# A tuned kernel for a long convolution and a linear attention block: other chunks, another transpose of the filter, 16-tile stages, work on GpSimd, and a new order

## The chip, the cores and the metric

The kernel runs on one core of one Trainium2 chip. The metric is the device time of one launch in microseconds (us). Engines are called as in the profile: PE (TensorE), DVE (VectorE), ACT (ScalarE), POOL (GpSimd) and SP (SyncE, which issues the DMAs). All data is bf16, and PE adds up in f32 in PSUM, which has eight banks.

## The reference

Two independent blocks share one output of 2048 x 1152, A in the left half and B in the right half. S = 2048 positions, D = 576 channels.

```python
k_shift = sum(k_pad[:, t:t + S, :] * shift_k[:, ks - 1 - t] for t in range(4))    # A: a 4-tap convolution
kv = k_shift * v
y = irfft(rfft(kv, 2 * S) * rfft(ssm_k, 2 * S))[:S]                               # a causal convolution of length S
a = q * (y + kv * ssm_D)
q, k, v = split(x @ wqkv)                                                         # B: 32 heads of 18 channels
pq, pk = phi(q), phi(k)          # phi(t) = t + 1 if t > 0 else exp(t), + 1e-6
o = (pq @ (pk^T v)) / (pq . sum(pk) + 1e-6)                                       # for each head
b = o @ wo
```

## The kernel before, in words

**Order.** Every piece of work is an `Op` with a number, registered by `P.op` in program order. `PLAN` (line 811) then lists all operations with the engine that runs each (P, A, D, G, S for PE, ACT, DVE, POOL, SP); `_issue` (104) and the loop at 793 to 805 issue them in that order, so each engine works through its list in order, and an operation that waits holds up what is behind it on its engine. `PLACES` fixes the SBUF offset or PSUM bank of every buffer. All DMAs go through `dma` (239) on the one SP queue, in order too. The costs given to `P.op` and the `bias` have no effect once the list is fixed.

**Block A.** The convolution over 4096 points is made of two small transforms, 128 by 16. `conv_piece` (373) makes kv on DVE in six pieces (three chunks of 192 channels, two halves of the positions): two products of 3,072 elements per partition (L383), additions (388, 391) and the product with v (394). `h_piece` (405) loads the filter 96 channels at a time, turns it on PE (416) and adds D (425). `s1` (434) is the first transform: for the filter (h) and for kv (u), per chunk four groups of matmuls with the table Gsb (445), each evicted by `copy` (246 to 250, so L248 is ACT and L250 is DVE) to Ch or Cu. `s2` (458) takes 64 channels (nine groups): a 32x32 block transpose on DVE (463), then two groups of eight 32x32 matmuls (476), each evicted to `sph` or `spu`. `inv` (492) swaps the even and odd partitions of the filter's spectrum by two DMAs (X), makes two products on DVE (500, 503), and then runs the inverse small transform on 32x32 tiles (513), evicted to V. `inv2` (525) writes V to DRAM in two halves (320 and 256 channels) and reads it back in another order, each half by 16 DMAs of 160 or 128 KB (540); the last matmuls use the table Esb (550), DVE multiplies by q (555), and four DMAs store each half.

**Block B.** x is loaded and turned by eight DMA transposes (299, 302) in four groups of 512 positions, xT. `kproj` (569) makes 128 rows of k by ten matmuls of 288 columns (577), an exponential on ACT (582), and phi on DVE (585). `qproj` (590) makes q transposed in chunks of seven heads, 126 channels, and a last one of 72 (599, 603, 606), to pqT. x is loaded again as x_sb (621), and `b_G` (630) computes G = x^T pk by 160 matmuls (636), from which kv and z of each head follow (673, 689); M = kv wo for each chunk of heads (732). The denominator goes over `dmm` (705) and a reciprocal on DVE (723); `b_bc` (740) spreads it by matmuls (747) and DVE multiplies pqT by it in ten operations (753). `b_out` (759) multiplies pqT by M, ten matmuls for 128 rows (766), evicts to `ob` and stores.

```python
    for b, p in zip([b for b in P.bufs if b.space != "dram"], places, strict=True):
        b.pos = p
...
            o.fn(o.eng)
```

Of the kernel before, what the change touches and what calls it, by code (L numbers as in the profile page):

```python
# [13 lines left out]
S = 2048  # L14
# [4 lines left out]
HEADS = [7, 7, 7, 7, 4]  # L19
CC = 192  # L20
NCC = 3
PCH = 64
VN = (320, 256)
VP = (0, 5)
HALF = 288

# [92 lines left out]
def _tables():  # L119
# [11 lines left out]
    pp = np.arange(128)  # L131
    k2p = 32 * (pp % 4) + pp // 4
    phe = ((4 * k2p[:, None, None] - 1) * n.T[None, :, :]) % 8192
# [21 lines left out]

    C = np.zeros((128, 96 + 128 + 630 + 32 + 160 + 126 + 8), np.float32)
    o = 0
    C[:, 0:96] = np.tile(W.reshape(32, 96), (4, 1))
    o = 96
    C[:, o:o + 128] = np.eye(128)  # L160
    o += 128
    es = np.zeros((32, 5, 126), np.float32)
    hm = np.zeros((128, 5, 32), np.float32)
    for c, (h0, hn) in enumerate(HCH):
        for m in range(hn):
            es[7 * c + m // 18, c, m] = 1.0
            hm[m, c, 7 * c + m // 18] = 1.0
    C[:, o:o + 630] = np.tile(es.reshape(32, 630), (4, 1))
    o += 630
    C[127, o:o + 32] = 1.0  # L170
    o += 32
    C[:, o:o + 160] = hm.reshape(128, 160)
    o += 160
    m = np.arange(126)
    C[:126, o:o + 126] = (m[:, None] // 18 == m[None, :] // 18)
    o += 126
    C[:, o:o + 8] = EPS
# [30 lines left out]
def kernel(  # L208
# [22 lines left out]
    V_d = [nc.dram_tensor("v_scr%d" % i, (128, 32 * VN[i]), BF, kind="Internal").ap() for i in range(2)]  # L231
# [39 lines left out]
    pqT = SB("pqT", [128, 5, S], side=1, pre=True)  # L271
# [8 lines left out]
    esel = lambda: cs(224, 630).rearrange("p (c m) -> p c m", c=5)  # L280
    sel127 = lambda: cs(854, 32)
    hmask = lambda: cs(886, 160).rearrange("p (c m) -> p c m", c=5)
    maskbd = lambda: cs(1046, 126)
    epsc = lambda: cs(1172, 1)

    P.op(("POOL", 0.1), lambda e: nc.gpsimd.memset(neg1.t[:], -1.0), wr=[neg1], name="neg1", bias=1000)
    for wx in (wk, wq):
        P.op(("POOL", 0.4), lambda e, wx=wx: nc.gpsimd.memset(wx.t[0:64, 4, :], 0.0), wr=[(wx, "z")], name="wz", bias=990)
        P.op(("POOL", 0.4), lambda e, wx=wx: nc.gpsimd.memset(wx.t[0:1, 4, :], 1.0), rd=[(wx, "z")], wr=[(wx, "z")],
             name="w1", bias=980)  # L290

    xTg = []

    def xt_load(g):
        b = SB("xT%d" % g, [128, 5, 512])
        xTg.append(b)

        def f1(e):
            nc.sync.dma_start_transpose(out=b.t[:, 0:4, :], in_=x[512 * g:512 * g + 512, 0:512])  # L299

        def f2(e):
            nc.sync.dma_start_transpose(out=b.t[:, 4:5, :], in_=x[512 * g:512 * g + 512, 448:576])
        load("xT", b, f1, 524288, wr=[(b, "m")], issue=3.3, row=256)
        load("xTt", b, f2, 131072, wr=[(b, "t")], issue=1.25, row=256)
        P.op(("POOL", 0.6), lambda e: nc.gpsimd.memset(b.t[0:1, 4, :], 1.0), rd=[(b, "t")], wr=[(b, "t")],
             name="xT1", bias=900)
# [13 lines left out]
    khs, vs = [], []  # L320

    def kv_load(bh):
        b0 = 8 * bh
        kh = SB("kh%d" % bh, [128, 11, D])
        vt = SB("v%d" % bh, [128, 8, D])
        khs.append(kh)
        vs.append(vt)
        if bh == 0:
            P.op(("POOL", 1.0), lambda e: nc.gpsimd.memset(kh.t[0:1, 0:3, :], 0.0), wr=[(kh, "z")], name="khz",
                 bias=970)  # L330
            for ci, (c0, cn) in enumerate(((0, CC), (CC, D - CC))):
                load("khh", kh, lambda e, c0=c0, cn=cn: dma(kh.t[1:16, 0:3, c0:c0 + cn], ap(
                    k, 13 * D + c0, [[16 * D, 15], [D, 3], [1, cn]])), 90 * cn, wr=[(kh, (ci, "h1"))], row=2 * cn)
                load("khh", kh, lambda e, c0=c0, cn=cn: dma(kh.t[16:128, 0:3, c0:c0 + cn], ap(
                    k, 253 * D + c0, [[16 * D, 112], [D, 3], [1, cn]])), 672 * cn, wr=[(kh, (ci, "h2"))],
                     row=2 * cn)
                load("kh0", kh, lambda e, c0=c0, cn=cn: dma(kh.t[:, 3:11, c0:c0 + cn], ap(
                    k, c0, [[16 * D, 128], [D, 8], [1, cn]])), 2048 * cn, wr=[(kh, (ci, "m"))], row=2 * cn)
        else:
            load("kh1", kh, lambda e: dma(kh.t[:], ap(k, 5 * D, [[16 * D, 128], [D, 11], [1, D]])), 1622016,  # L340
                 wr=[(kh, "m")])
        load("v%d" % bh, vt, lambda e: dma(vt.t[:], ap(v, b0 * D, [[16 * D, 128], [D, 8], [1, D]])), 1179648, wr=[(vt, "v")])
# [16 lines left out]
    kv_load(0)  # L359
    xt_load(0)  # L360
# [6 lines left out]
    load("Gsb", Gsb, lambda e: dma(Gsb.t[:].rearrange("p a b c -> p (a b c)"), G_d), 1048576)  # L367
    load("Drow", Drow, lambda e: dma(Drow.t[:], A_ssm_D.rearrange("(o d) -> o d", o=1)), 1152)


    m = SB("m", [128, 4, 8, CC])

    def conv_piece(cc, bh):
        kh, vt = khs[bh], vs[bh]
        c0 = cc * CC

        def tap(e, i):
            base = kh.t[:, i:i + 8, c0:c0 + CC]
            i0 = bass.AP(tensor=base.tensor, offset=base.offset,
                         ap=[list(base.ap[0]), [D, 2], [D, 8], [1, CC]])  # L380
            w = Wj.t[:, 2 - i:4 - i, c0:c0 + CC]
# [500 lines left out]
```

## Time and profile before

| what | value |
|---|---|
| median of 3 runs (lowest, highest) | 198.97 us (196.22, 200.73) |
| span of the profiled execution, first to last instruction | 197.3 us |
| mean granted PE clock in it | 0.895 |
| ACT, POOL busy | 120.0 us, 6.9 us |
| DMA | 39.49 MB, mean 200 GB/s |

The profile records one execution. Its own time as the runs count it isn't given apart from the span; the median of the runs lies 1.7 us above the span. Busy is the time in which an engine had an instruction at work. A group line gives the source line, the engine, the operation, output <- input, the shape, the count, the busy time, the mean of one in ns, and the idle time of the engine just before the group with what ended it. A chain line gives start, duration and what it was.

### The profile page before, as it was taken

The numbers are of one execution on the slowest core, as the hardware profiler recorded it, in microseconds if no ns is written. First come the engines' busy times: TensorE is split into PE (matmuls) and PEld (weight loads), VectorE is DVE, ScalarE is ACT, GpSimd is POOL, SyncE is SP. The second block draws the span as 40 slices with busy tenths as digits, with TensorE's granted clock in tenths as the row PEclk, the third lists the DMA queues.
The fourth block names the chain that finished last, engine by engine and source line by source line (L and its number), as shares of the span: only waits on it lengthen the run. The fifth ranks groups of instructions, "written<-read, shape, count | busy, mean of one in ns | idle before, by whom it ended". The sixth has DMA issues, their size and how long they took to land.

```text
span 197.3 us, 3955 instructions
## 1 busy us (share of the span) xinstructions
PE 162.8 (83%) x1664; PEld 108.2 (55%) x1664; DVE 153.4 (78%) x150; ACT 120.0 (61%) x127; POOL 6.9 (3%) x18
## 2 busy tenths in 40 slices
PE   0985999938999999889998897798779999996820
PEld 0763576627666675668775564362233566774610
DVE  0477599999799999999954999979899548482650
ACT  2293566595767576997524699979998583201100
POOL 8010100020010000000000000000000000000000
PEclk9996699985999999999999999769555699999996
DMA  6999899996013680209950021930699789967696
GB/s 182 348 171 262 307 379 382 300 230 138 0 22 118 201 279 17 92 3 278 372 233 0 3 106 69 308 108 0 257 342 257 187 240 360 354 189 211 198 323 185
DMA packets 40536, 39.49 MB, mean 200 GB/s; under 512 B 13575, under 2 KB 37765, under 8 KB 39622
## 3 DMA queue, kind: packets, MB, share of 16 engines
q1 hardware_dynamic: 40518, 39.24, 64.7%
q8 instruction: 13, 0.21, 0.5%
q14 instruction: 5, 0.04, 0.1%
HBM read 22.46 MB, written 9.44 MB: 162 GB/s over the span
## 4 chain that ended last, share of the span: by engine, by line
PE 37%; DVE 24%; ACT 12%; SPq 11%; issue 7%; DMA 6%; DVEq 1%; ACTq 0%
PE ps_all L636 8%; SPq L240 7%; PE ps_all L599 6%; PE ps_all L577 6%; PE ps_all L766 6%; DVE m L383 5%; PE ps_all L445 5%; DMA Vt<-v_scr 3%; ACT Cu L248 3%; DVE X L500 3%; SPq L299 2%; DVE pk L585 2%; DVE ct L463 2%; DMA wk<-in_B_wqkv_dram 2%; PE ps_all L550 2%
## 5 line engine op out<-in xcount | busy, mean ns | idle before, releaser
L445 PEld LDWEIGHTS <-Gsb 128*128 128x128 bf16 x240 | 20.0, 113 | 11.2 <-issue 9.7
L577 PE MATMUL ps_all<-wk,xT 128*128 128x288 bf16 x160 | 23.4, 306 | 2.5 <-DMA wk<-in_B_wqkv_dram 2.5
L766 PE MATMUL ps_all<-M,pqT 126*128 126x288 bf16 (+1 forms) x160 | 23.5, 305 | 0.2 <-ACT V L248 0.2
L599 PE MATMUL ps_all<-xT,wq 128*126 128x512 bf16 (+1 forms) x100 | 23.5, 386 | 0.1
L383 DVE TENSOR_TENSOR m<-kh,Wj 128x3072 bf16<-128x3072 bf16 x12 | 20.7, 1750 | 1.9 <-DMA kh<-in_A_k_dram 1.9
L577 PEld LDWEIGHTS <-xT 128*128 128x128 bf16 x160 | 16.4, 104 | 9.3 <-issue 3.6
L766 PEld LDWEIGHTS <-pqT 126*128 126x128 bf16 (+1 forms) x160 | 16.4, 103 | 7.5 <-issue 2.2
L636 PE MATMUL ps_all<-pk,x_sb 128*128 128x288 bf16 (+1 forms) x160 | 20.4, 286 | 0.1
L248 ACT ACTIVATE sph<-ps_all 128x1024 bf16<-128x1024 f32 x16 | 16.2, 1028 | 4.4 <-PE ps_all L476 4.4
L248 ACT ACTIVATE spu<-ps_all 128x1024 bf16<-128x1024 f32 x16 | 15.9, 1028 | 4.7 <-PE ps_all L476 4.7
L248 ACT ACTIVATE Cu<-ps_all 128x1536 bf16<-128x1536 f32 x12 | 17.5, 1502 | 1.1 <-PE ps_all L445 1.0
L582 ACT ACTIVATE ek<-ps_all,neg 128x576 bf16<-128x576 f32 x16 | 11.8, 741 | 10.5 <-PE ps_all L577 6.9
L636 PEld LDWEIGHTS <-x_sb 128*128 128x128 bf16 x160 | 15.5, 98 | 4.8 <-issue 0.9
L599 PEld LDWEIGHTS <-wq 128*126 128x126 bf16 (+1 forms) x100 | 13.1, 135 | 8.3 <-issue 1.3
L248 ACT ACTIVATE Ch<-ps_all 128x1536 bf16<-128x1536 f32 x11 | 16.1, 1523 | 2.5 <-PE ps_all L445 2.3
L248 ACT ACTIVATE ob<-ps_all 128x576 bf16<-128x576 f32 x10 | 6.5, 652 | 17.7 <-PE ps_all L766 17.3
L445 PE MATMUL ps_all<-hT,Gsb 128*128 128x192 bf16 (+2 forms) x120 | 12.8, 272 | 5.3 <-DVE hT L425 3.4
L476 PE MATMUL ps_all<-ct,cst 32*32 32x512 bf16 x288 | 13.2, 438 | 4.0 <-ACT Cu L248 0.9
L603 ACT ACTIVATE eq<-ps_all,neg 126x1024 bf16<-126x1024 f32 (+1 forms) x10 | 11.1, 1114 | 7.8 <-PE ps_all L599 7.8
L248 ACT ACTIVATE V<-ps_all 128x1024 bf16<-128x1024 f32 x14 | 13.7, 1035 | 2.7 <-PE ps_all L513 2.7
L555 DVE TENSOR_TENSOR q<-ps_all,q 128x640 bf16<-128x640 f32 (+1 forms) x12 | 11.0, 953 | 5.5 <-PE ps_all L550 4.6
L585 DVE SCALAR_TENSOR_TENSOR pk<-ek,ps_all 128x576 bf16<-128x576 bf16 x16 | 11.6, 746 | 3.7 <-ACT ek L582 2.0
(69 smaller groups left out, 224.1 us busy)
## 6 DMA issues: line engine op xcount, KB each, us to landing
X<-sph SPq DMA_DIRECT2D x18, 256.0 KB, 2.8
v_scr<-V SPq DMA_DIRECT2D x1, 2560.0 KB, 10.0
Vt<-v_scr SPq DMA_DIRECT2D x16, 160.0 KB, 3.5
hs<-in_A_ssm_k_dram SPq DMA_DIRECT2D x6, 384.0 KB, 5.6
v<-in_A_v_dram SPq DMA_DIRECT2D x2, 1152.0 KB, 11.1
x_sb<-in_B_x_dram SPq DMA_DIRECT2D x1, 2304.0 KB, 9.5
out_dram<-ob SPq DMA_DIRECT2D x16, 144.0 KB, 3.3
v_scr<-V SPq DMA_DIRECT2D x1, 2048.0 KB
```

The lines of the kernel that those rows point to most:

```text
L240: nc.sync.dma_start(out=dst, in_=src)
L248: nc.scalar.activation(out=o, in_=i, func=ACTF.Copy)
L383: nc.vector.tensor_tensor(out=m.t[:, i:i + 2], in0=i0, in1=i1, op=ALU.mult)
L445: nc.tensor.matmul(ps.t[:, bank, lo - 512 * bank:hi - 512 * bank], lhsT=Gsb.t[:, b, ri, :], rhs=src[:, lo - CC * j:hi - CC * j], start=Tru ...
L476: nc.tensor.matmul(ps.t[32 * j:32 * j + 32, kk, :].rearrange("p (k w t) -> p w k t", w=8, t=2), lhsT=W2()[32 * kh:32 * kh + 32, :], rhs=ct ...
L577: nc.tensor.matmul(ps.t[:, hh, 0:HALF], lhsT=xT.t[:, t, 128 * (r % 4):128 * (r % 4) + 128], rhs=wk.t[:, t, HALF * hh:HALF * hh + HALF], st ...
L582: P.op(("ACT", _act(576) + 0.085), lambda e: nc.scalar.activation(out=eb.t[:], in_=ps.t[:, :, 0:HALF], func=ACTF.Exp, bias=neg1.t[:]), rd= ...
L585: P.op(("DVE", _dve(576)), lambda e: nc.vector.scalar_tensor_tensor(out=pk.t[:, r, 0:D].rearrange("p (h c) -> p h c", h=2), in0=eb.t[:], s ...
L599: nc.tensor.matmul(ps.t[0:hn, j, :], lhsT=wq.t[:, t, h0:h0 + hn], rhs=xT.t[:, t, :], start=(t == 0), stop=(t == 4))
L603: P.op(("ACT", _act(1024) + 0.09), lambda e: nc.scalar.activation(out=eb.t[0:hn], in_=ps.t[0:hn], func=ACTF.Exp, bias=neg1.t[0:hn, :]), rd ...
L636: nc.tensor.matmul(ps.t[:, hh, 0:n], lhsT=x_sb.t[:, r, FT[t]:FT[t] + 128], rhs=pk.t[:, r, HALF * hh:HALF * hh + n], start=(r == 0), stop=( ...
L766: nc.tensor.matmul(ps.t[:, hh, 0:HALF], lhsT=pqT.t[0:hn, c, 128 * r:128 * r + 128], rhs=M.t[0:hn, c, HALF * hh:HALF * hh + HALF], start=(c ...
```

## The change

- **x** (`x_load`, `xt_load`): x_sb is loaded at the start in four parts. Groups 0 and 1 of xT are turned on PE from x_sb (XPE = 2) and evicted by ACT or DVE; groups 2 and 3 still by DMA transposes.
- **Convolution**: pieces of 128 channels (HP), the last of 64; all four tap products in one instruction; k and v are kept in one buffer each.
- **Filter**: pieces of 128 channels. For pieces 1 to 4 (HDMA) the transpose between s1 and s2 is a DMA transpose from SBUF to SBUF, 512 KB for 64 channels (seven of them), followed by two times two matmuls over all 128 partitions (W2q); piece 0 keeps the block transposes on DVE. The filter's loads for these pieces permute channels.
- **16-tile stages**: s2 and i1 run their 32x32 matmuls over all 16 tiles of the array in one operation (16 and 32 matmuls).
- **Spectral products**: each may run on DVE or POOL; the new plan puts nine of eighteen on POOL.
- **Inverse**: V goes in groups of 256, 256 and 64 channels. The first two (DR) are evicted to U, written to DRAM and read back by four DMAs of 512 KB. The third has no DRAM trip: its inverse matmuls use the data as the stationary side (i1s), so that the result lies as i2 wants it.
- **Block B**: phi in halves (kproj by 288 columns, qproj by 512); q in chunks of 128 channels that straddle heads, the 64-channel tails of two position groups packed into one tile (pqt); M in six parts, each the sum of two head chunks; bc in nine parts, of which four (PQG) are copied out by ACT or DVE and multiplied on POOL, which also adds EPS (`pqe`); G and out evicted by halves.
- **Fillers**: `FILL` puts 62 matmuls of 256 columns over zeros ahead of chosen operations, into a bank that the operation writes afterwards.
- **Plan**: new PLAN and PLACES. SP's order starts with cst, srow, the first filter piece, Gsb, Drow, a part of wk, x (first part), the head of k, wk, k, v, x (second part), wq, k (second half), x (third), then xT of group 2.

The core of the diff (PLAN, PLACES and most repeated lines left out):

```diff
+HP = [(0, 128), (128, 128), (256, 128), (384, 128), (512, 64)]
+QG = [(0, 256), (256, 256), (512, 64)]
 HALF = 288
+XPE = 2
+HDMA = (1, 2, 3, 4)
+DR = (0, 1)
...
+        if g < XPE:
+            for t in range(5):
+                ps = psb(1, "xps") if t % 2 == 0 else ps
+                c0 = 128 * t if t < 4 else D - 128
+
+                def tr(e, t=t, ps=ps, c0=c0):
+                    o = ps.t.rearrange("p b c -> p (b c)").bitcast(BF)
+                    for j in range(4):
+                        nc.tensor.transpose(out=o[:, 512 * (t % 2) + 128 * j:512 * (t % 2) + 128 * j + 128],
+                                            in_=x_sb.t[:, 4 * g + j, c0:c0 + 128], identity=ident())
+                P.op(("PE", 4 * 0.065), tr, rd=[(x_sb, g), cst], wr=[(ps, t % 2)], use=[b], name="xtr", cnt=4,
...
+            w = Wj.t[:, 3:4, c0:c0 + n]
+            i1 = bass.AP(tensor=w.tensor, offset=w.offset, ap=[list(w.ap[0]), [-D, 4], [0, 8], [1, n]])
+            nc.vector.tensor_tensor(out=m.t[:], in0=i0, in1=i1, op=ALU.mult)
...
+            cq = SB("cq", [128, 16, S // 16])
+            P.op(("SP", 3.0), lambda e, g=g, cq=cq: nc.sync.dma_start_transpose(
+                out=cq.t[:], in_=C.t[:, 16 * g:16 * g + 16].rearrange("p w r t -> p (w r t)")),
+                rd=[C], wr=[cq], name="trq", tx=_dma(524288, 256), bias=(nm, 0.0))
+            for hh in range(2):
+                ps = psb(2, "s2ps")
+
+                def mm(e, hh=hh, ps=ps, cq=cq):
+                    for k in range(2):
+                        nc.tensor.matmul(ps.t[:, k, :], lhsT=W2q(), rhs=cq.t[:, 8 * hh + 4 * k:8 * hh + 4 * k + 4, :],
+                                         start=True, stop=True)
+                P.op(("PE", _pe(512, 512)), mm, rd=[cq, cst], wr=[ps], use=[sp], name="s2q", cnt=2, bias=(nm, 0.0))
...
+        ps = [psb(2, "s2ps") for _ in range(2)]
+
+        def mm(e):
+            for j in range(4):
+                for kh in range(4):
+                    nc.tensor.matmul(ps[kh // 2].t[32 * j:32 * j + 32, kh % 2, :], lhsT=W2()[32 * kh:32 * kh + 32, :],
+                                     rhs=ct.t[32 * kh:32 * kh + 32, 8 * j:8 * j + 8], start=True, stop=True)
+        P.op(("PE", T16), mm, rd=[ct, cst], wr=ps, use=[sp], name="s2" + sfx, bias=bias, cnt=16)
...
+        for x, wr in ((1, [(tx, ("x", 0)), (tx, ("x", 1))]), (0, [(tx, 0), (tx, 1)])):
+            P.op({"DVE": _dve(2048, 2), "POOL": TPOOL}, lambda e, x=x: (nc.vector if e == "DVE" else nc.gpsimd).tensor_tensor(
+                out=tx.t[:, x], in0=su.t[:], in1=tx.t[:, x], op=ALU.mult), rd=[su], wr=wr, name="p%d" % x, bias=bias)
+        c0 = PCH * (g % 4)
+        if vg in DR:
+            ps = [psb(2, "i1ps") for _ in range(2)]
+
+            def mm(e):
+                for wi, w in enumerate((W31, W32)):
+                    for kh in range(4):
+                        for j in range(4):
+                            nc.tensor.matmul(ps[j // 2].t[32 * kh:32 * kh + 32, j % 2, :].rearrange(
+                                "p (k w t) -> p w k t", w=8, t=2), lhsT=w()[32 * j:32 * j + 32, :],
+                                rhs=tx.t[32 * j:32 * j + 32, wi, :, 32 * kh:32 * kh + 32, :],
+                                start=(wi == 0), stop=(wi == 1))
+            P.op(("PE", 2 * T16), mm, rd=[tx, cst], wr=ps, use=[U[vg]], name="i1", bias=bias, cnt=32)
...
+                for q in range(8):
+                    o = ps.t[:, q // 4, 128 * (q % 4):128 * (q % 4) + 128]
+                    for x, w in ((0, W31q), (1, W32q)):
+                        nc.tensor.matmul(o, lhsT=tx.t[:, x, 4 * hh + q // 2, :, q % 2], rhs=w(), start=(x == 0),
+                                         stop=(x == 1))
+            P.op(("PE", 16 * 0.065), mm, rd=[tx, cst], wr=[ps], use=[V[vg]], name="i1s", bias=bias, cnt=16)
...
+            load("Vw", None, lambda e: dma(ap(V_d[vg], 0, [[32 * n, 4], [128 * n, 32], [1, 32 * n]]),
+                                           U[vg].t[:].rearrange("p k c -> p (k c)")), 8192 * n, rd=[U[vg]],
+                 wr=[dtok], bias=bias, row=8192)
+            for bq in range(4):
+                load("Vr", V[vg], lambda e, bq=bq: dma(V[vg].t[:, 8 * bq:8 * bq + 8, :], ap(
+                    V_d[vg], 8 * bq * 128 * n, [[n, 128], [128 * n, 8], [1, n]])), 2048 * n, rd=[dtok],
+                    wr=[(V[vg], bq)], bias=bias, row=2 * n)
...
-                vt = SB("Vt", [128, 8, n])
-                for kh in range(4):
-                    load("Vr", vt, lambda e, b4=bg * nb, vt=vt, kh=kh: dma(
-                        vt.t[kh:128:4], ap(vd, (32 * kh + 2 * b4) * 32 * n, [[n, 32], [32 * n, 8], [1, n]])),
-                        512 * n, rd=[dtok], wr=[(vt, kh)], bias=bias, row=2 * n)
...
+            P.op(("ACT", _act(HALF) + 0.085), lambda e, hh=hh, ps=ps: nc.scalar.activation(
+                out=eb.t[:, hh], in_=ps.t[:, 0, 0:HALF], func=ACTF.Exp, bias=neg1.t[:]), rd=[ps, neg1], wr=[(eb, hh)],
+                 name="kexp", bias=("k", 0.0))
...
+            for t in range(5):
+                if c < 4:
+                    nc.tensor.matmul(ps.t[:, 0, :], lhsT=wq.t[:, t, 128 * c:128 * c + 128],
+                                     rhs=xTg[g].t[:, t, :], start=(t == 0), stop=(t == 4))
+                else:
+                    for i in range(2):
+                        nc.tensor.matmul(ps.t[64 * i:64 * i + 64, 0, :], lhsT=wq.t[:, t, TL:D],
+                                         rhs=xTg[2 * i + g].t[:, t, :], start=(t == 0), stop=(t == 4))
...
+                for i, (w, lo) in enumerate(src):
+                    hn = HCH[min(w, 4)][1]
+                    nc.tensor.matmul(ps.t[:, hh, 0:HALF], lhsT=kvb.t[0:hn, w, lo:lo + 128],
+                                     rhs=wo5.t[0:hn, min(w, 4), HALF * hh:HALF * hh + HALF], start=(i == 0),
+                                     stop=(i == len(src) - 1))
...
+        if (c, gp) in PQG:
+            bb = SB("bb", [128, 2, 512])
+            P.op(either(1024), lambda e: copy(e, bb.t[:], ps.t[:]), rd=[ps], wr=[bb], name="bcev", bias=("bc", 0.0))
+            P.op(("POOL", TPQ), lambda e: nc.gpsimd.tensor_tensor(
+                out=pq(c, gp), in0=pq(c, gp), in1=bb.t[:], op=ALU.mult), rd=[bb], wr=wr,
+                name="pqg", bias=("bc", 0.0))
+            return
...
+            for b in [b for b in o.bufs if b.space == "ps"][:1]:
+                for _ in range(fill.get(o.id, 0)):
+                    nc.tensor.matmul(b.t[:, 0, 0:256], lhsT=fz.t[:, 0:128], rhs=fz.t[:], start=True, stop=True)
...
+TPOOL = 4.9
+TPQ = 2.6
+TPE = 1.3
+PQG = ((0, 0), (1, 0), (0, 1), (1, 1))
+YB = 8
```

## The prediction

> **What bounds the kernel now.** I read the totals first, then the slices, then a table of stages, the waits of the DMA queue and the chain.
>
> ```profile
> PE 162.8 (83%) x1664; PEld 108.2 (55%) x1664; DVE 153.4 (78%) x150; ACT 120.0 (61%) x127; POOL 6.9 (3%) x18
> ...
> DVE  0477599999799999999954999979899548482650
> ...
> DMA  6999899996013680209950021930699789967696
> ```
>
> DVE and PE are both busy for most of the span; POOL is free. DVE's digits are low at the start, in the middle (slices 18 and 19) and at the end.
>
> ```profile
> 0.00:17.20 17.20, 8.54 (x77) 6.83 (x78) 7.85 (x9) 8.93 (x7) 4.55 (x13) 0.97 0.90 245
> 20.00:90.00 70.00, 63.64 (x532) 44.40 (x531) 65.40 (x63) 50.95 (x53) 2.30 (x5) 0.93 0.58 179
> 90.00:112.00 22.00, 21.23 (x235) 15.54 (x234) 16.75 (x18) 10.82 (x15) 0.00 (x0) 1.00 0.52 179
> 112.00:161.40 49.40, 42.80 (x627) 22.27 (x627) 43.47 (x41) 43.98 (x47) 0.00 (x0) 0.76 0.58 181
> 161.40:197.30 35.90, 23.84 (x187) 17.43 (x185) 18.11 (x20) 5.09 (x8) 0.00 (x0) 0.95 0.81 259
> ```
>
> Third number on: busy PE, PEld, DVE, ACT, POOL, then clock, DMA share, GB/s. I cut at 161.4, where the last part of V is evicted: up to there DVE is 93% busy once k is under way (idle 4.6, 5.2 and 5.9 us in the three middle rows, 15.8 in all), so the middle is DVE's. After it DVE is busy 18.11 of 35.90 us: another bound.
>
> ```profile
> SPq L240 <- DMA v_scr<-V: 10.2, 2, 8.9
> ```
>
> ```profile
> 178.53 2.58 DMA Vt<-v_scr
> ...
> 186.69 2.36 DVE q L555 x2
> ```
>
> ```profile
> 171.99 9.13 SPq L240 DMA_DIRECT2D Vt<-v_scr  x14
> ...
> 192.76 0.86 SPq L240 DMA_DIRECT2D out_dram<-ob  x1
> ```
>
> These are SP's own waits (total, times, longest), the end of the chain, and SP's timeline. The tail is a round trip through DRAM: write of V (8.9 us for 2,048 KB), then 16 reads that the one SP queue issues at about 0.6 us each, landing, product, stores. SP ends its last issue at 193.62.
>
> ```profile
> L463 DVE STREAM_TRANSPOSE ct<-Ch 128x1024 f32<-128x1024 f32 x9 | 10.7, 1222 | 0.4 <-ACT Ch L248 0.4
> L500 DVE TENSOR_TENSOR X<-spu,X 128x2048 bf16<-128x2048 bf16 x9 | 10.8, 1213 | 0.0
> L582 ACT ACTIVATE ek<-ps_all,neg 128x576 bf16<-128x576 f32 x16 | 11.8, 741 | 10.5 <-PE ps_all L577 6.9 <-issue 3.3
> L655 POOL MEMSET wv<- 128x576 bf16 x1 | 0.6, 582 | 15.2 <-PE ps_all L599 15.2
> ```
>
> ```profile
> L383 DVE TENSOR_TENSOR m<-kh,Wj x12: 1737/1750/1758, 11.0 to 86.5; 128x3072 bf16<-128x3072 bf16 x12
> L299 SPq DMA_TRANSPOSE xT<-in_B_x_dram x4: 2686/4190/4892, 5.7 to 43.6; - x4
> ```
>
> These, from the groups by form and from single lines (min/median/max ns), are prices: a 32x32 block transpose, a spectral product, an exponential, a POOL memset, a convolution product, and the SP time of a 512 KB DMA transpose.
>
> **The change, part by part.** DVE is priced first, by mean duration times count. From the rows, a two-tensor bf16 op costs 156 ns + 0.519 ns per element (1,536 in 953, 3,072 in 1,750), an f32 PSUM read 143 ns + 1.05 per element (576 in 746, 1,024 in 1,215).
> - Convolution: 30 instructions (12, 6, 6, 6) of 43 us become 40; a 128-channel piece is 2.28+1.22+0.69+0.69 = 4.88, a 64-channel piece 2.75: 8x4.88+2x2.75 = 44.5 us, +1.7.
> - Filter turned by DMA: 7 of 18 block transposes go, 7x1.22 = -8.5.
> - Spectral products: the new plan puts 9 of 18 on POOL, 9x1.21 = -10.9. Of ten normalisings 4 go to POOL and one disappears (tails packed into one tile): -6.0, +1.2 for one copy that DVE makes for POOL.
> - Halved tiles: 32 kphi of 288 at 0.445 = 14.2 (+2.3); 18 qphi of 512 at 0.68 = 12.2 (0); 18 output products of 512 = 12.2 (+0.8); 12 half oev against 6 whole, +0.9.
> - Straddling chunks: M has 6 evictions for 5 and bc 9 for 10, all full height; the first on ACT, the second counted above. A memset of kvb more on POOL, before anybody waits for it.
> - The plan moves evictions from ACT: 9 s1 of 1,024 and 4 of 512 for one of 1,536, +12; two s2ev and two i1ev more, +4.9; small ones, about -0.7.
>
> Sum: 161.5 us of durations now, 159.3 after. Busy time is less than durations because neighbours overlap: (161.5-153.4)/150 = 55 ns each. After, 192 instructions give 159.3-10.6 = 148.7. What counts is the part ahead of the last eviction of U1, which releases the last round trip: now 7.85+127.39 = 135.2 us by 161.4; in the new order 171 instructions of 145.1 us stand ahead of it, 145.1-9.4 = 135.7. The same work, so the gain must come from idle time.
>
> ACT: half exponentials at 0.50 (fixed part 0.26 us from 576 in 741 and 1,024 in 1,116) make 16.0 of 11.8 us; 32 s1 or s2 pieces shift as above; its durations come to 130 us, now 120. It stays below DVE, so I cost it at nothing; without DVE as cover it costs these 10 us.
>
> PE: x transposes 40x84 ns (the row of hT's transposes) +3.4; 62 fillers of 256 columns at 0.127 us +7.9; 28 filter matmuls of 512 columns at 0.235 +6.6 for 112 small ones at 46 ns -5.2; inverse stage with 16 tiles at once, up to -6; q tail, 20 of 0.23 paired, -2.3; 10 more M, 32 more output matmuls, 80 more s1 loads, about +6. Near +10 us on 162.8, under 94% of the time below, cover DVE. Fillers stand where PE waits; wrongly placed they cost up to 7.9.
>
> **Start.** SP now issues constants, one filter piece, Gsb, x and wk before k and v; x is turned on PE, so two of four pairs of DMA transposes (4.19 us of SP each) leave the head. Ahead of the first k rows stand 4.9 MB; slice one moved 0.9 MB, slice two ran at 348 GB/s: 4.9+4.0/0.348 = 16.4, say 17 us. DVE has 6.7 us done by then, so it starts its unbroken run 10.3 us behind its own work. First k projection can start when wk is in, 3.7 MB: about 13 us (now 17.18). The x loads moved up here were hidden in the middle; now they stand ahead of the second half of k, which lands after 8.5 MB, 17+3.6/0.348 = 27 us, against its first use on DVE at 29 (12 us of DVE work after 17). If they bring it later, DVE waits.
>
> **Middle.** Of 15.8 us of idle time I let go: 5.2 in the G stage (the new order puts 20 convolution instructions beside G, where DVE now has 18 instructions of all kinds), 2.7 of 5.4 us of waits for exponentials (pk and pqT; halved tiles), and 2.3 of 4.5 for s2, i1 and bc on PE (16 tiles at once). 5.6 stays. New waits:
> - Seven SBUF transposes of 512 KB queue on SP with the X loads, Esb and wo between them. Bounds 7x2.7 = 19 to 7x4.9 = 34 us; at the median 29. They start when the s1 pieces of the filter are out, near 93 us (82 us of DVE work stand ahead, plus 10.3), and X3, X6 and X7 queue behind: at 29 us the swap for the product p1 of group 3 lands near 129 us against its turn on DVE at 127 (112 us of work less overlap, plus start and the idle time before it). I take 2.5; 0 to 8.
> - POOL: no row shows a POOL product. Memsets write 1.01 ns per element (576 in 582): one write 2.1 us for 2,048, three passes 6.2; I take 4.1, two passes. Nine make 37 us, four normalisings and their additions some 12. Where a DVE product and a POOL product meet, no row shows what happens; the nearest, a POOL memset of 514 ns beside L383, leaves that at 1,737 to 1,758. Bounds: nothing, to the full time of POOL beside such DVE work: 4 products in the convolution (16.4) and about 6 later. I take two products caught, 8.2. i1 is queued on PE behind them, and s1, out and i2 behind i1.
>
> [...]
>
> Middle in all: 5.6+2.5+8.2 = 16.3 us of idle time.
>
> **Tail.** U1 written: 0.6 issue, 8.9; four reads in place of sixteen: 0.6, then 2.1 MB at the 259 GB/s of the last stage, 8.1; last two products 2x0.44 on PE and 0.68 on DVE, 1.8 with starts; 0.6 issue, and 3.7 from SP's last issue to the end, as now. 24.3 against 35.9. The third group of 64 channels makes no trip; it is turned with the data as the stationary side, 32 matmuls whose price I take from hT's transposes. Of SP's 56 issues after 149 us some 30 remain, 18 us at 0.6, so SP no longer sets this. PE has 16 half rows of out (5x0.147 each, 11.8), twelve products i2 of four (0.52 each, 6.2), i1s (2.7) and the third group's i2 (2.6) behind the last i1: 23 us, nearly as long, so the tail can't be below that; 28 if DMA goes at 200 GB/s.
>
> **Sum.** 10.3+135.7+16.3+24.3 = 186.6 us of span, against 197.3. The median of the runs is 198.97, 1.7 above the profiled span (what lies around it isn't shown separately): 188.3 us.
>
> **Rivals.**
> - *The idle time stays.* Nothing in the middle is released and the new waits are added: 15.8 for 5.6, 198.5. For: waits in the middle are many and small, none above 2.5. Against: G has cover. 192 to 203, chance 0.18.
> - *DVE and POOL exclude each other.* Place: the four products beside the convolution, then those beside p1 and p0. All 22 us for 8.2 is 202; POOL at 6.2 us each makes it 33, 213. It is slower by over 2% from 23 us on. [...] Against: POOL would often wait, not DVE. Chance 0.14.
> - *Everything hidden.* No POOL or queue waits: 188.3-10.7 = 177.6; range 175 to 182, chance 0.12. For: POOL has 45 us for its last 33.
> - Forecast, 182 to 195: 0.56.
>
> **Numbers.** About 2% is what a measurement of this kernel can tell: under 195.0 faster, over 202.9 slower. Faster: 0.56 + 0.12 + 0.04 of the first rival = 0.72; same: 0.13 of it and 0.04 of the second = 0.17; slower the rest, 0.11. Range 177 to 203, from all hidden to full exclusion; own range of the forecast 182 to 195.
>
> **What would show it.** First k near 13 us and unbroken DVE from 17; convolution products at 2.28 us (stretched beside POOL means exclusion); POOL products near 4.1; DVE busy near 149; SP free between Vr reads; 24 us from U1's last eviction to the end. Wrong if DVE isn't the middle's bound: if it idles over 20 us between 17 and U1, or PE waits for POOL ahead of i1.

## The result and the profile after

The changed kernel takes 249.69 us (median of 4 runs), the kernel before 199.85 us on the same chip: a ratio of 1.262 [1.241, 1.283]. Some executions of a kernel run over a per cent longer than the rest; the ratios leave them out (so they differ a little from the quotient of the medians), and of e7 and b5, which were profiled in such an execution, only durations and shares are read. The profiled span is 245.8 us. The prediction was 188.3 us, a span of 186.6; the span is 59.2 us longer than that.

The page of the kernel after, its totals, the slices of DVE and DMA, and the chain by line:

```profile
PE 168.9 (69%) x1777; PEld 113.6 (46%) x1787; DVE 175.2 (71%) x192; ACT 124.2 (51%) x173; POOL 71.4 (29%) x37
...
DVE  0179998999999988979899999799600794000352
...
DMA  5999998993390000199997932243227834222895
...
DMA v_scr<-U 26%; PE ps_all L700 7%; DVE m L413 5%; DMA kb<-in_A_k_dram 5%; PE ps_all L501 4%; DMA V<-v_scr 3%; PE ps_all L611 3%; DMA Gsb<-tab_g 3%; DVE pk L650 3%; DVE pqT L673 3%; DVE v L424 3%; DMA xT<-in_B_x_dram 2%; DVE m L418 2%; PE ps_all L644 2%; PE ps_all L662 2%
```

Two things differ from what was forecast. DVE is busy 175.2 us (forecast: 148.7). And two holes have come into DVE's slices, at slices 30 and 31 and 35 to 37, with DMA at two tenths beside four of the five: a kernel that waits for a DMA that uses few of the engines. A quarter of the chain is `v_scr<-U`, the two writes of U to DRAM.

The same kernel by stages, cut at the start of DVE's unbroken run, at 100, at the issue of the first write of U, at its end, and at the eviction that releases the second (columns as in the prediction's table):

```profile
0.00:20.50 20.50, 14.41 (x124) 11.04 (x125) 7.01 (x10) 9.86 (x12) 6.30 (x16) 1.00 0.90 285
20.50:100.00 79.50, 65.03 (x526) 42.67 (x530) 76.59 (x94) 46.08 (x76) 20.59 (x8) 0.91 0.59 150
100.00:152.20 52.20, 44.66 (x643) 29.70 (x644) 49.02 (x47) 45.43 (x52) 23.48 (x8) 1.00 0.81 183
152.20:184.80 32.60, 14.49 (x193) 8.61 (x191) 22.05 (x17) 12.52 (x19) 16.93 (x5) 0.86 0.29 86
184.80:195.40 10.60, 6.34 (x106) 3.54 (x106) 3.63 (x5) 2.96 (x3) 0.00 (x0) 0.61 0.82 250
195.40:245.80 50.40, 23.94 (x208) 18.06 (x205) 16.92 (x22) 7.38 (x14) 4.05 (x1) 0.75 0.52 153
```

Against the four terms of the forecast:

| term | forecast | measured, from the rows | difference |
|---|---|---|---|
| start (time less DVE's own work) | 10.3 | 20.50 - 7.01 = 13.5 | +3.2 |
| DVE work ahead of U1's last eviction | 135.7 | 7.01 + 76.59 + 49.02 + 22.05 + 3.63 = 158.3 | +22.6 |
| DVE idle in between | 16.3 | 174.9 - 151.3 = 23.6 | +7.3 |
| tail | 24.3 | 50.4 | +26.1 |
| span | 186.6 | 245.8 | +59.2 |

23.0 us of the tail's 26.1, and 15.0 us of the idle time, are the write. The chain of the kernel after (start, duration, what):

```profile
152.17 32.55 DMA v_scr<-U
184.77 4.24 DMA V<-v_scr
189.06 1.89 PE ps_all L611 x8
190.94 1.01 PE ps_all L558 x31
...
195.64 31.93 DMA v_scr<-U
...
227.66 3.92 DMA V<-v_scr
```

Both writes carry 2,048 KB and take 32 us, 65 GB/s; the forecast had 8.9. The last 12.7 us of the first one, when nearly nothing else moved, against the stretch of a write in the kernel before:

```profile
172.00:184.70 12.70, 2.11 (x42) 0.94 (x22) 3.98 (x3) 2.69 (x5) 1.76 (x1) 0.77 0.23 83
```

```profile
162.90:172.00 9.10, 8.69 (x69) 6.49 (x68) 6.36 (x7) 2.03 (x4) 0.00 (x0) 1.00 0.99 368
```

The last two numbers are the DMA share and GB/s. 0.23 of 16 engines is 3.7 engines' worth, 83 GB/s; before it was 0.99 and 368. The DMA records of the traces show the same row by row: of the write's rows of 16 KB, on average 3.8 are in flight at a time in the kernel after and never more than 6; in the kernel before it is 11 on average and up to 17.

The waits of the kernel after show what stood behind. In PE's order the i1 of U1's last groups (L558, at 190.94 in the chain above) sits behind the i2 of the first read (L611, at 189.06):

```profile
PE ps_all L611 <- DMA V<-v_scr: 32.7, 2, 17.8
...
DVE q L621 <- PE ps_all L611: 21.8, 7, 15.0
```

DVE's 22.6 us more (26.5 over the whole span) are in five groups, all of instructions with two inputs in SBUF. Groups by form of the kernel after, with the unstretched L413 of 4,096 elements beside them:

```profile
L548 DVE TENSOR_TENSOR TT<-su,TT 128x2048 bf16<-128x2048 bf16 x9 | 25.0, 2790 | 0.0
L413 DVE TENSOR_TENSOR m<-kb,Wj 128x4096 bf16<-128x4096 bf16 x8 | 18.3, 2288 | 0.3 <-DMA kb<-in_A_k_dram 0.2
...
L413 DVE TENSOR_TENSOR m<-kb,Wj 128x2048 bf16<-128x2048 bf16 x2 | 6.3, 3136 | 0.0
...
L418 DVE TENSOR_TENSOR m<-m 128x1024 bf16<-128x1024 bf16 x2 | 5.1, 2557 | 0.0
L424 DVE TENSOR_TENSOR v<-m,v 128x512 bf16<-128x512 bf16 x2 | 4.7, 2344 | 0.0
L421 DVE TENSOR_TENSOR m<-m 128x512 bf16<-128x512 bf16 x2 | 2.5, 1269 | 0.0
```

A product of 4,096 elements costs 2,288 ns, as forecast, and one of half the size 3,136: the smaller is the dearer. The spectral products cost 2,790 for 1,213. The timeline of the kernel after says why; POOL, then DVE:

```profile
67.03 18.46 POOL L548 TENSOR_TENSOR TT<-su,TT 128x2048 bf16<-128x2048 bf16 x4 [18.67 <-ACT su L255]
```

```profile
66.73 1.20 DVE L413 TENSOR_TENSOR m<-kb,Wj 128x2048 bf16<-128x2048 bf16 x1
67.96 4.44 DVE L418 TENSOR_TENSOR m<-m 128x1024 bf16<-128x1024 bf16 x1
72.31 0.67 DVE L673 SCALAR_TENSOR_TENSOR pqT<-eq,ps_all 128x512 bf16<-128x512 bf16 x1
...
74.47 2.11 DVE L421 TENSOR_TENSOR m<-m 128x512 bf16<-128x512 bf16 x1
76.51 5.08 DVE L413 TENSOR_TENSOR m<-kb,Wj 128x2048 bf16<-128x2048 bf16 x1
81.51 4.26 DVE L424 TENSOR_TENSOR v<-m,v 128x512 bf16<-128x512 bf16 x1
85.70 0.68 DVE L418 TENSOR_TENSOR m<-m 128x1024 bf16<-128x1024 bf16 x1
```

Four POOL products fill 67.0 to 85.5 us. Inside that stretch each DVE instruction with two SBUF inputs takes some part of a POOL product (4.5 us) longer, save the one at 66.73 that had begun before POOL, while phi (L673), with one input in PSUM, takes 0.67 (0.64 to 0.69 over all 18 in the run). The first instruction after it, at 85.70, is back at 0.68.

### The profile page after: what moved, and what is told of

Read it like the earlier page. It is cut to its first block, busy times and chain, and to the rows that moved or that the text cites. A ratio compares the mean times of both kernels' runs of the same rounds, so it can differ in the third digit from the quotient of the medians.

```text
span 245.8 us, 4335 instructions
## 1 busy us (share of the span) xinstructions
PE 168.9 (69%) x1777; PEld 113.6 (46%) x1787; DVE 175.2 (71%) x192; ACT 124.2 (51%) x173; POOL 71.4 (29%) x37
## 4 chain that ended last, share of the span: by engine, by line
DMA 39%; PE 23%; DVE 22%; issue 6%; ACT 6%; SPq 1%; DVEq 0%; ACTq 0%
DMA v_scr<-U 26%; PE ps_all L700 7%; DVE m L413 5%; DMA kb<-in_A_k_dram 5%; PE ps_all L501 4%; DMA V<-v_scr 3%; PE ps_all L611 3%; DMA Gsb<-tab_g 3%; DVE pk L650 3%; DVE pqT L673 3%; DVE v L424 3%; DMA xT<-in_B_x_dram 2%; DVE m L418 2%; PE ps_all L644 2%; PE ps_all L662 2%
## 5 line engine op out<-in xcount | busy, mean ns | idle before, releaser
L548 POOL TENSOR_TENSOR TT<-su,TT 128x2048 bf16<-128x2048 bf16 x9 | 40.6, 4524 | 47.7 <-issue 24.3
L611 PE MATMUL ps_all<-V,Esb 128*128 128x256 bf16 x64 | 11.3, 338 | 32.7 <-DMA V<-v_scr 32.7
L861 PE MATMUL ps_all<-M,pqT 128*128 128x288 bf16 x128 | 23.9, 319 | 8.5 <-DVE ob L257 6.8
L700 PEld LDWEIGHTS <-x_sb 128*128 128x128 bf16 x160 | 17.4, 110 | 18.0 <-issue 11.5
L548 DVE TENSOR_TENSOR TT<-su,TT 128x2048 bf16<-128x2048 bf16 x9 | 25.0, 2790 | 0.0
L413 DVE TENSOR_TENSOR m<-kb,Wj 128x4096 bf16<-128x4096 bf16 (+1 forms) x10 | 24.6, 2457 | 0.3 <-DMA kb<-in_A_k_dram 0.2
L611 PEld LDWEIGHTS <-Esb 128*128 128x128 bf16 x64 | 7.3, 118 | 36.5 <-issue 19.1
L845 POOL TENSOR_SCALAR pqT<-pqT 128x1024 bf16<-128x1024 bf16 x4 | 11.1, 2770 | 43.1 <-DVE TT L257 42.8
L861 PEld LDWEIGHTS <-pqT 128*128 128x128 bf16 x128 | 13.2, 107 | 15.3 <-issue 9.1
L662 PE MATMUL ps_all<-xT,wq 128*128 128x512 bf16 x74 | 18.6, 379 | 0.4
L255 ACT ACTIVATE TT<-ps_all 128x1024 bf16<-128x1024 f32 x15 | 18.0, 1261 | 0.9 <-PE ps_all L484 0.9
L909 PE MATMUL ps_all<-fz 128*128 128x256 bf16 x62 | 11.8, 303 | 8.7 <-POOL fz L889 4.4
L647 ACT ACTIVATE ek<-ps_all,neg 128x288 bf16<-128x288 f32 x32 | 15.4, 507 | 3.3 <-PE ps_all L644 2.5
L255 ACT ACTIVATE su<-ps_all 128x1024 bf16<-128x1024 f32 x15 | 14.8, 1022 | 3.1 <-PE ps_all L527 3.0
```

What stands on the lines that cost most here:

```text
L255: nc.scalar.activation(out=o, in_=i, func=ACTF.Copy)
L413: nc.vector.tensor_tensor(out=m.t[:], in0=i0, in1=i1, op=ALU.mult)
L548: P.op({"DVE": _dve(2048, 2), "POOL": TPOOL}, lambda e, x=x: (nc.vector if e == "DVE" else nc.gpsimd).tensor_tensor(out=tx.t[:, x], in0=su ...
L611: nc.tensor.matmul(ps.t[:, 0, n * j:n * j + n], lhsT=Esb.t[:, b, ri, :], rhs=v_, start=(ri == 0), stop=(ri == 1))
L647: P.op(("ACT", _act(HALF) + 0.085), lambda e, hh=hh, ps=ps: nc.scalar.activation(out=eb.t[:, hh], in_=ps.t[:, 0, 0:HALF], func=ACTF.Exp, b ...
L662: nc.tensor.matmul(ps.t[:, 0, :], lhsT=wq.t[:, t, 128 * c:128 * c + 128], rhs=xTg[g].t[:, t, :], start=(t == 0), stop=(t == 4))
```

## The experiments

Eleven more kernels ran; each ratio is to the kernel before on the same chip. e1 to e3 and b4 ran on one chip, e5 to e7 and b5 on another, e8 to e10 on a third.

| run | what | us | ratio [95%] |
|---|---|---|---|
| after | the change | 249.69 | 1.262 [1.241, 1.283] |
| e1_split | write of U in four DMAs | 211.75 | 1.072 [1.062, 1.082] |
| e2_dve | all products on DVE | 236.73 | 1.200 [1.186, 1.214] |
| e3_both | both | 196.14 | 0.992 [0.987, 0.997] |
| b4_lead4 | before, with such a write | 254.92 | 1.290 [1.278, 1.301] |
| e5_nofill | e3, no fillers | 195.53 | 0.976 [0.968, 0.984] |
| e6_normdve | e3, normalising on DVE | 198.90 | 0.993 [0.988, 0.998] |
| e7_late5 | e1, early four products on DVE | 200.72 | 1.005 [1.002, 1.009] |
| b5_read4 | before, with the new round trip | 200.40 | 1.003 [0.997, 1.009] |
| e8_best | e5 and e6 together | 199.17 | 0.993 [0.985, 1.001] |
| e9_memset | e1, four products as memsets | 197.73 | 0.990 [0.984, 0.996] |
| e10_copy | e1, four products as copies | 204.98 | 1.024 [1.018, 1.030] |

The theory had two parts: the write of U runs on a quarter of the DMA engines because its outermost dimension in DRAM (the first count of its access pattern) is 4, and POOL's products lock DVE out. The rivals were that the write is slow for its scattered addresses, and that DVE or PE loses its time to something else.

**The write: e1_split** (the diffs here are shortened):

```diff
-            load("Vw", None, lambda e: dma(ap(V_d[vg], 0, [[32 * n, 4], [128 * n, 32], [1, 32 * n]]),
-                                           U[vg].t[:].rearrange("p k c -> p (k c)")), ...
+            def vw(e):
+                for a in range(4):
+                    dma(ap(V_d[vg], 32 * n * a, [[128 * n, 32], [1, 32 * n]]),
+                        U[vg].t[32 * a:32 * a + 32].rearrange("p k c -> p (k c)"))
```

> The changed kernel, with each of the two writes of U to DRAM issued as four DMAs of 32 partitions (512 KB each) in place of one whose DRAM pattern has an outermost dimension of 4; the same rows go to the same addresses, and all else is as it was. Theory A (the outermost dimension of 4 confines the write to 4 of 16 DMA engines): each write takes about 9 us in place of 32 (32.55 and 31.93 on the chain), DMA share near 1 while it runs in place of 0.23, and the time falls by 40 to 46 us to about 204. Theory B (the rows are scattered in DRAM, 128n elements apart, and that is slow): no change, 250. Theory C (DVE and POOL excluding each other is the main loss): the writes are a small part; the time falls by under 20 us.

211.75 us, 38 less. The same rows go to the same addresses, so the addresses are not the cause of these 38 us; what changed is that each DMA's outermost dimension is 32. In the DMA records 14 of the 16 KB rows are now in flight on average. The gain is a little under the 40 to 46 expected: each write takes 12.9 us from its issue to the first read's (152.28 to 165.20, 179.68 to 192.56), not 9.

**The write by itself: b4_lead4**, in the kernel before, where nothing is scattered:

```diff
-dma(vd, V[hf].t[:].rearrange("p k c -> p (k c)"))
+dma(ap(vd, 0, [[1024 * n + 64, 4], [32 * n, 32], [1, 32 * n]]), V[hf].t[:].rearrange("p k c -> p (k c)"))
```

Between the four blocks lie 64 unused elements, so that the dimension of 4 stays one of its own; the reads skip them.

> The kernel before, with its two writes of V to DRAM through a pattern with an outermost dimension of 4 (four blocks of 32 partitions, 64 unused elements between blocks, read back accordingly); no row is scattered. Theory A: 2,560 KB and 2,048 KB at the 65 GB/s that the changed kernel's writes had are 40 and 32 us in place of 10 and 9, the second queued behind the first on the same engines; the time rises by 35 to 50 us, to 235 to 250. Theory B (scatter): no change, 199.

254.92 us, 1.29 times before, a little above the range expected. The chain of that run:

```profile
140.17 41.17 DMA v_scr<-V
...
194.39 33.72 DMA v_scr<-V
```

Four long runs of addresses in order, and still 34 to 41 us, with a DMA share of 0.25 between 160 and 180 us and on average 3.6 to 3.9 of the write's rows in flight. So an outermost dimension of 4 alone makes the loss. With it the share was 0.23 in the kernel after and 0.25 here, about a quarter of the 16 engines, with fewer than four rows in flight on average; the kernel before, with 128, had 0.99 and 11.

**The products: e2_dve and e3_both.** The plan's nine `G` of products become `D` at the same places; e3 takes the split write too.

> The changed kernel with its nine POOL spectral products on DVE, at the same places of the order; the writes are left as they were. Theory C (a DVE instruction with two SBUF inputs and a POOL instruction that reads SBUF exclude each other): the 27 us by which DVE's products are stretched go, nine products of 1.21 us come, DVE busy falls from 175 to about 159, and the time falls by 15 to 20 us to about 232, since the stretch beside the convolution (67 to 87 us) lies on the chain. Rival (POOL was a help and the stretched products were covered): the time rises by up to 11 us.

> Both edits: writes in four DMAs and all nine products on DVE. If theories A and C are both right and their prices add, 250 less 43 less 17, about 190, faster than the kernel before and near the 188.3 predicted. If the two losses cover each other, above 200.

e2 took 13 us off, e3 53.6: the two causes (38 and 13) add up to within 3 us and leave 196. Both fell short of their expectations, 15 to 20 us less and a time of about 190. In e2 the groups by form are back at their price, the spectral products nearly so, since POOL still normalises:

```profile
L548 DVE TENSOR_TENSOR TT<-su,TT 128x2048 bf16<-128x2048 bf16 x18 | 23.8, 1350 | 0.0
...
L413 DVE TENSOR_TENSOR m<-kb,Wj 128x2048 bf16<-128x2048 bf16 x2 | 2.4, 1201 | 0.0
...
L418 DVE TENSOR_TENSOR m<-m 128x1024 bf16<-128x1024 bf16 x2 | 1.3, 673 | 0.0
```

**Which products: e7_late5.** e1 with only the four of groups 0 and 1, beside the convolution, given to DVE (`G536 G537 G547 G548` become `D`).

> e1_split with only the four early POOL products (groups 0 and 1, beside the convolution) moved to DVE; the other five stay on POOL. Theory C: the loss lies where DVE runs products with two SBUF inputs; the early four cost 17 us beside the convolution and 4.9 us as DVE work, so most of the 15.6 us between e1_split and e3_both comes back: 198 to 202. Rival (the loss is spread evenly over the nine): four ninths of it, about 205.

200.72, within the 198 to 202 expected. Of the 15.6 us between e1 and e3 these four are 11.0 by the times and 13 by the ratios (1.072 less 1.005, of 199; the run was on another chip than e1 and e3), the five late ones the rest, 3 to 5. DVE's groups account for most of both. The four early products spare DVE 4 x 1.21 = 4.8 us and stretch its convolution by 13.3 (2.4 expected of L413's row with two for 6.3, 1.3 for 5.1, 0.8 for 4.7, 0.8 for 2.5): 8.5 net. The five late ones spare 6.1 and stretch the spectral products by 14.1 (25.0 less 9 x 1.21), 3.0 of which e3 has too, from normalising on POOL (24.3, against 21.3 in e6, which has none): 5.0 net. DVE's busy time says the same: 174.0 us in e1, 165.6 in e7, 160.6 in e3.

**What POOL does to DVE: e9_memset and e10_copy.** Both are e1 with the same four POOL products replaced, so that DVE's own work is e1's. They leave out four of the eighteen spectral products.

```diff
-nc.gpsimd.tensor_tensor(out=tx.t[:, x], in0=su.t[:], in1=tx.t[:, x], op=ALU.mult)
+[nc.gpsimd.memset(tx.t[:, x], 0.25) for _ in range(2)]      # e9: writes only
+nc.gpsimd.tensor_copy(out=tx.t[:, x], in_=su.t[:])          # e10: reads one input
```

> The kernel with the split write, in which the four early products on POOL (groups 0 and 1) are each replaced by two memsets of the same tile: POOL is as long busy at the same places (about 2.1 us a memset, 4.2 for 4.5), but writes only. This leaves out four of the eighteen spectral products. Theory 'what excludes is reading SBUF': DVE's convolution products keep 2.29, 1.22 and 0.69 us beside it and the time is that with the four on DVE less their DVE work, 196 to 201 us. Rival 'POOL's being busy on SBUF at all, or the wait for POOL's result, costs the time': DVE stretched as with the products, 209 to 213 us.

> The same place, but POOL copies the filter's 2,048 bf16 elements into the tile (one input in SBUF in place of two). This leaves out four of the eighteen spectral products. Theory 'any POOL instruction that reads SBUF excludes a DVE instruction with two SBUF inputs': DVE's products beside the copies are stretched, each by up to the length of a copy, and the time lies between that of memsets and that of products, in proportion to a copy's length. Rival 'only POOL instructions with two SBUF inputs exclude': DVE keeps 2.29 us and the time equals that with memsets.

The memsets did not run at the products' places, as expected of them: with no input they did not wait for `su`, and ran from 49.2 us on. But there, too, DVE's convolution went on beside them. POOL, then DVE, of e9:

```profile
49.15 14.47 POOL L548 MEMSET TT<- 128x2048 bf16 x8
```

```profile
50.99 0.68 DVE L424 TENSOR_TENSOR v<-m,v 128x1024 bf16<-128x1024 bf16 x1
...
51.95 2.29 DVE L413 TENSOR_TENSOR m<-kb,Wj 128x4096 bf16<-128x4096 bf16 x1
...
55.84 1.23 DVE L418 TENSOR_TENSOR m<-m 128x2048 bf16<-128x2048 bf16 x1
```

None of them is stretched. In e10 the copies (2,379 ns each) ran at the products' place, and DVE beside them shows the same picture as in the kernel after, at half the size:

```profile
67.59 2.65 POOL L548 COPY TT<-su 128x2048 bf16<-128x2048 bf16 x1 [18.70 <-ACT su L255]
71.97 6.75 POOL L548 COPY TT<-su 128x2048 bf16<-128x2048 bf16 x3 [1.72 <-ACT su L255]
```

```profile
68.52 2.27 DVE L418 TENSOR_TENSOR m<-m 128x1024 bf16<-128x1024 bf16 x1
...
74.06 2.91 DVE L413 TENSOR_TENSOR m<-kb,Wj 128x2048 bf16<-128x2048 bf16 x1
76.89 2.11 DVE L424 TENSOR_TENSOR v<-m,v 128x512 bf16<-128x512 bf16 x1
78.92 0.68 DVE L418 TENSOR_TENSOR m<-m 128x1024 bf16<-128x1024 bf16 x1
```

The times: 197.73 with memsets, 204.98 with copies, 211.75 with products. Copies against memsets, on the same chip, are 7.3 us dearer; that is 0.52 of the step from memsets to products by the times and 0.41 by the ratios (e1 ran on another chip), and a copy lasts 2.38 / 4.52 = 0.53 of a product. The rival that PE's wait for POOL's results made the time, since the memsets were also done earlier, is answered by DVE's own work: it is busy 160.8 us with memsets, 166.5 with copies and 174.0 with products, which is 13.2 of the 14.0 us from memsets to products and 5.7 of the 7.3 from memsets to copies. One input read from SBUF was enough (2.27 and 2.91 us beside the copies, where L418 and L413 took 0.69 and 1.22 in e9), and the price went roughly by how long POOL read.

**What is left over: e5, e6, e8, b5.** With both causes mended the kernel stands at 196, not 188. Four runs asked where the 8 us are.

e5 leaves the 62 fillers out of e3 (`FILL` empty):

> e3_both (writes in four DMAs, all eighteen products on DVE) without the 62 filler matmuls. Theory (DVE is the bound of the middle, PE has room): within 2 us of e3_both's 196. Rival (the fillers keep the granted clock up): the mean clock falls from 0.966 towards the 0.895 of the kernel before, and the time rises by 3 to 5 us.

195.53, a ratio of 0.976 [0.968, 0.984], the lowest of all these kernels. The fillers did not hold the clock up: the granted clock of the profiled execution is 0.961 without and 0.966 with them. Against e3, on another chip, leaving them out gives 0.6 us by the times and 3 by the ratios.

e6 normalises all parts on DVE straight from PSUM in e3 (the copy, the POOL addition and the POOL product go):

> e3_both with the four POOL normalisings undone: DVE multiplies straight from PSUM at the place of the copy, no copy on ACT, no POOL addition, no POOL product. DVE gets three products of 1.21 (the fourth replaces its copy), 3.6 us; in e3_both POOL's normalising stretched three spectral products from 1.21 to 2.4, 2.3 and 3.0 us, 4.1 us in all, which go. Theory (exclusion takes back what POOL saves): within 2 us of 196. Rival (POOL normalising is a help): 3 to 4 us slower than e3_both.

0.993: the same time as e3. All 18 spectral products take 1.20 to 1.22 us. In e3, with normalising on POOL, two of them were stretched, to 2.4 and 3.0 us, 3.0 in all (the expectation counted three and 4.1). That pays for about the extra work of DVE and no more.

> Both causes mended, no fillers, normalising on DVE straight from PSUM, nothing on POOL that reads SBUF. If what separates the normalisings on POOL from those on DVE and what the fillers cost add up: 194 to 196 us, ratio to the kernel before 0.965 to 0.98, DVE's 18 products of 2,048 all at 1.20 to 1.22 us. If DVE's extra work of four normalisings is on the path: 196 to 198.

A miss: the two together came to 0.993, not 0.965 to 0.98. Against e6, with fillers and otherwise alike, nothing is gained (198.90, 199.17). So what the fillers cost stays open between nothing and 3 us, and so does whether e5 keeps its 2.4% on another chip.

b5 puts one part of the change alone into the kernel before: V is written by four DMAs of 32 partitions with interleaved rows, and each half is read by four DMAs in place of sixteen, with the rows of Esb reordered to match.

```diff
-vt.t[kh:128:4], ap(vd, (32 * kh + 2 * b4) * 32 * n, [[n, 32], [32 * n, 8], [1, n]])
+vt.t[:], ap(vd, 2 * b4 * 128 * n, [[n, 128], [128 * n, 8], [1, n]])        # for one kh of four
```

> [...] Theory (in the tail the SP queue's issues count): 24 issues of 0.6 us go and 6 come, about 7 us of them on the last round trip: 190 to 193. Rival (the DMA engines carry the tail, not SP): 197 to 200.

200.4, no gain. The stage of the tail in that run:

```profile
163.00:200.00 37.00, 27.00 (x224) 19.81 (x200) 19.19 (x21) 7.30 (x11) 0.00 (x0) 0.91 1.02 287
```

The DMA engines are full (1.02, against 0.81 in the last stage of the kernel before), and the queue's issues have become dearer, 5.46 us for four reads in SP's timeline. But the run does not price the fewer issues by themselves, since the write changed with them. From its issue to the first read the write takes 12.7 us (166.1 to 178.8) where the old one took 9.1 (162.9 to 172.0); from there to the end 22.1 us pass, where it was 25.3. What the reads gain the write takes back, and the round trip as a whole gains nothing.

## Why the prediction was wrong, step by step

With both causes taken out, e3's trace has the forecast's own terms again. Stages of e3, then its chain after the last write:

```profile
0.00:20.00 20.00, 14.62 (x115) 11.62 (x116) 6.18 (x9) 9.11 (x11) 6.30 (x16) 1.00 0.88 277
20.00:100.00 80.00, 73.75 (x701) 51.86 (x705) 78.51 (x111) 54.94 (x88) 2.13 (x4) 1.00 0.66 173
100.00:164.70 64.70, 53.55 (x775) 31.22 (x776) 61.69 (x62) 52.45 (x62) 20.35 (x8) 0.95 0.83 206
...
164.70:195.40 30.70, 21.04 (x208) 16.77 (x192) 14.19 (x23) 7.48 (x14) 0.00 (x0) 0.90 0.95 255
```

```profile
177.47 5.05 DMA V<-v_scr
182.56 1.87 PE ps_all L613 x8
184.43 1.90 PE ps_all L863 x10
...
189.43 0.69 DVE q L623
```

- **"U1 written: 0.6 issue, 8.9" failed**, and with it most of the forecast. The price came from another pattern: the old write's outermost dimension was 128, the new one's is 4, and the diff shows it. (The 8.9 was also misread: it is SP's wait for the first old write, of 2,560 KB. The one of 2,048 KB took 9.1 from its issue to the first read, so by luck the number fits.) It measured 31.9 us in the tail, and the first write, which the sum had hidden behind DVE's work, added 15.0 of idle time. e1 took 38 us off by the pattern alone, and b4 put more than that onto the kernel before. The prediction's own sign of being wrong, DVE idle for over 20 us between 17 and U1, came up through it: 23.6.
- **"I take two products caught, 8.2" failed** in size and in place. The rival for it named the mechanism and the place ("the four products beside the convolution, then those beside p1 and p0") but gave it 0.14. It appeared as longer DVE instructions, not as idle time: 27.4 us of stretch by the groups above, 23.9 of it ahead of U1's last eviction, more than the 22 that the prediction took as the most. With it DVE's work there was 158.3 us for 135.7. The row that I had weighed against it, a memset beside L383, could not speak: a tap product of 4,096 elements kept its 2.29 us beside memsets (e9), and one of 2,048 took 2.91 for 1.22 beside copies, which read (e10). Net of the DVE work that the products on POOL spared, the loss is 13 us (e2) to 15.6 (e1 against e3), most of it at the four early products.
- **POOL product 4.1**: median 4.50, within its bounds.
- **DVE work ahead of U1's last eviction, 135.7: right, to within 2 us.** In e3 eight of the nine products are back on DVE ahead of it (the ninth, at 167.58, comes after): 135.7 + 8 x 1.21 less their overlap of 0.4 is 145.0, and 6.18 + 78.51 + 61.69 is 146.4, of which 3.0 are stretch by the normalising on POOL. The piecewise prices held (2.28 for a tap product: 2,288).
- **The middle's idle time, 5.6 + 2.5: near.** e3 has 144.7 - 140.2 = 4.5. In the kernel after, 23.6 less the 15.0 for the write leaves 8.6. G did get its cover.
- **Seven DMA transposes, 29 us**: six took 19.31 and the seventh 3.81 in SP's timeline of the kernel after, 23.1, and nothing on the chain waited for them.
- **Start, DVE unbroken from 17: late.** The first k projection began at 17.4, not near 13, the last of the first half of k landed at 20.5, and the start cost 13.5 (13.8 in e3) for 10.3.
- **Tail without the slow write, 24.3: 30.7 in e3.** The write took 12.7 from its issue to the first read (164.8 to 177.5) for 9.5; reads and the products behind them 12.6 for 10.5; the end 5.3 for 4.3. Other stores beside the write are not why it is longer: DMA was as busy in it as in the old write (1.00 and 0.99), but moved 244 GB/s for 368, and by the DMA records its rows of 16 KB last 1.27 us for 0.61 (medians). Whether the split into four DMAs or the interleaved rows do that is open; the single write of the kernel after has the interleaved rows too, at 0.67 to 0.76. "SP no longer sets this" is not refuted: in b5 the part from the first read on did become shorter. DMA runs at a share of 0.95 in e3's last stage, which speaks for the bytes as its bound; no run with fewer bytes was made.
- **Fillers "where PE waits"**: they cost nothing to 3 us (e5, e8), under the 7.9 that wrong places would have cost.
- **A reading that nothing rests on**: DVE's low digits in the middle of the kernel before are slices 21 and 22, not 18 and 19.

So e3's span follows from the forecast's: 186.6, less 8.2 for products no longer caught, plus 10.7 of work back on DVE, +3.5 in the start, -3.6 of idle time, +6.4 in the tail: 195.4. These are differences read from e3's rows, and show where the forecast was off.

Against the kernel before (9.4 at the start, 135.2 of DVE work, 16.8 idle, 35.9 of tail) e3 has 12.3 us less idle time and 5.2 less tail, as the forecast hoped in kind, but 11.2 more DVE work ahead of U1 and 4.5 more at the start. The forecast's list has 16.9 us of evictions moved from ACT to DVE, which the products on POOL were to balance; with the products back on DVE that balance is gone.

## What to carry to other kernels

In these runs a DMA's price went by its access pattern, not only by its bytes: 2,048 KB took 9.1 us with an outermost dimension of 128 in DRAM, 32 to 34 with 4, and 12.7 to 13.1 as four DMAs of 32. Look at that dimension, and take a row's price only if it has the same. Before work is moved to POOL, look at what DVE runs beside it: in these runs a POOL instruction that read SBUF held up the DVE instructions with two SBUF inputs beside it (4.44 us for 0.68 beside a product of 4.5) and not those with one in PSUM (phi, 0.67), so it belongs, if anywhere, beside DVE work that reads PSUM. A resource that a row shows undisturbed by one kind of instruction (here a memset) is not shown free for another kind.

## What the runs showed of the hardware

- A write of 2,048 KB with an outermost dimension of 4 took 32 to 34 us (32.55 and 31.93 in the kernel after, 33.72 in b4; 2,560 KB: 41.17 in b4) at a DMA share of 0.23 to 0.26, with 3.6 to 3.9 of its rows in flight; as four DMAs of 32 partitions the same write took 12.7 to 13.1 us in e1 and e3, with 14 rows in flight (e1) that lasted 1.27 us each (e3) for 0.61 in the kernel before.
- DVE instructions with one input in PSUM were not stretched beside POOL (L673 of the kernel after, 0.67 us), nor were those with two SBUF inputs beside POOL memsets (e9: 2.29, 1.23 and 0.68 us).
- POOL's instructions were stretched as well: its product of two tensors of 1,024 bf16 elements took 2,128 ns in e2, and 3,100 in the kernel after beside a DVE product with two SBUF inputs (POOL from 143.07 us on, DVE from 141.37 to 144.19).
- A one-input addition of 1,024 bf16 elements took POOL 2,770 ns (L845, kernel after), longer than that product (2,128 in e2) and than its copy of 2,048 (2,379 in e10).
- DMA transposes from SBUF to SBUF of 512 KB held SP for 3.2 us each in the kernel after (six in 19.31 us) and for 2.9 in e3 (six in 17.30).
- In the kernel after the first eight matmuls of L611, after a wait of 14.95 us, took 1.89 us at a granted clock of 0.50 (189.06 to 190.95); eight of the same shape from 194.08 on took 1.05, at 1.00. In e3's tail, after a wait of 3.45 us, the first eight (L613) took 1.87 us and the next eight 1.04.
